# Strassen's seven products also for the last four column blocks of the value matrix, and a ring of output rows one slot shorter

## The chip, the cores and the metric

The kernel runs on one core of a Trainium2 chip. A core has five engines that run their own instruction queues side by side: TensorE (PE; its weight loads are listed as PEld), VectorE (DVE), ScalarE (ACT), GpSimd (POOL) and SyncE (SP, which here issues DMAs). The metric is device time in microseconds (us) of one execution, the median of several runs.

## What is computed

Eight batches, eight heads, 576 positions, head size 64; then a gated layer over 4608 tokens of 512 features, with 1536 hidden features:

```python
scores = q @ k.T / sqrt(64)                  # per batch and head
ret    = scores * Dmat                       # Dmat: gamma_h ** (i - j) for i >= j, else 0
attn   = ret @ v
x      = attn, tokens x 512
gate   = 1 / (1 + exp(-(x @ w_gate)))
val    = x @ w_val
out    = (gate * val) @ w_out
```

The inputs are float32; the kernel multiplies in bfloat16 and adds in float32.

## The kernel before

**The tokens.** The attention is made in steps of 128 tokens. Its output x, transposed, is handled by the gated layer in blocks: 512 tokens at the start, two blocks of 256 (512 and 768 in `BLOCKS`), and seven blocks of 512 from token 1024 on. The change concerns these seven. While the gated layer of one block runs, the attention steps of the next are put between its products.

**The order.** The program is scheduled by hand (`manual_schedule`): each engine takes its instructions in the order in which the program issues them, and an instruction waits by semaphore until its inputs are there and until whatever still reads the place it writes is done.

**Strassen in a 512-token block.** The 1536 hidden features are three units (`u` = 0, 1, 2) of four column blocks of 128 each. For a unit, the product of 512 tokens, 512 features and 512 columns is a 2 x 2 product of quarters. With Strassen's scheme (Winograd's form) it takes seven quarter products instead of eight. A quarter product (`quarter`, `product`, the matmuls on L967) is four matmuls of 128 x 128 by 256 columns. The text names it by kind, unit and number: g16 is gate, unit 1, product 6; w is the value. The two weight-side sums and the difference that a unit needs (`w_sums`) and the token-side sums (`x_sums`) are made ahead.

A unit's products run through three PSUM banks, "a", "g" and "e" (`BANKS`). What happens to them (`quarter`):

- 1 goes into a; ScalarE copies a into g (L994). 2 adds into g, and g leaves as the first quarter of the result.
- 6 adds into a; ScalarE copies a away as u2 (L949). 5 goes into e; ScalarE copies e away as s5 (L949).
- 3 adds into e; VectorE adds e to u2 (L1002). That result leaves as another quarter.
- 7 adds into a; VectorE adds a to s5 (L1005). That result leaves as another quarter.
- 4 adds into a once more, and a leaves as the last quarter.

"Leaves" (L988, L990) is for the gate a sigmoid on ScalarE into the tile `gv`, and for the value a multiplication of `gv` in place: on VectorE where it comes from a bank (products 2 and 4), on GpSimd where it comes from u2 or s5 (products 3 and 7). The leaving of 3 and 7 is put into the list `waiting` and issued only behind the matmuls of the next product, ahead of that product's own work (`settle`).

**Plain products.** Before the change, all three units of the gate and the first two of the value are made like this. The last four column blocks of the value (8 to 11) are made plainly by `value(fc)`: per column block four matmuls of 512 columns (L1016) and one VectorE multiplication (L1019).

**The order of a block** is written out in `ORDER`. Behind a colon stand the sums of finished `gv` quarters (`gsum`) that the output product needs: "0", "1", "2" on VectorE (L909), "t" on GpSimd (L903), and "a", "b" for one half of a unit, four sums each, all on GpSimd. Three quarter products of a block are issued early, in the block before (`EARLY`).

**The output product** (`quarters`, L1074) is again seven products, of 12 matmuls of 256 columns each (1.31 us). The first begins as soon as `ORDER` is through. Behind it comes a group of two attention steps (`slot_of_two`). In it VectorE's two tiny `glance` copies (L698) separate the two halves of the attention values in the same banks: TensorE may begin the second half only behind them. VectorE then masks the next scores (L643).

**Rings.** `ffn_psum` hands out three PSUM banks and `osb` 13 places of 128 x 512 float32, least recently used first; three of the `osb` places are held for weight sums of the value (`value_sums_begin`). Finished output rows wait in `osb`; up to `keeps` = 6 of them stay before the oldest is sent (`stored`, `leave`). `weight_sums` lists the weight-side sums that are issued one by one during the two 256-token blocks, and `PLACES` the in-place differences issued later.

Of the kernel before, what the change touches and what calls it, by code (L numbers as in the profile page):

```python
# [9 lines left out]
FP32 = mybir.dt.float32  # L10
BF16 = mybir.dt.bfloat16
AF = mybir.ActivationFunctionType
ALU = mybir.AluOpType
# [3 lines left out]
def kernel(  # L17
# [19 lines left out]
    nc = tc.nc  # L37
# [4 lines left out]
    P = 128  # L42
    M = H // 2
    NC = (S + P - 1) // P
    NKC = DM // P
    NFC = DFF // P
# [18 lines left out]
    class Ring:  # L65
# [4 lines left out]
            self.held = []  # L70
            self.partly = set()

        def tile(self, shape, dt, tag, name, written=False):
            i = next(x for x in self.order if x not in self.held and not (written and x in self.partly))
            self.partly.discard(i)
            if name.startswith("row"):
                self.partly.add(i)
            self.order.remove(i)
            self.order.append(i)
            self.last = i  # L80
            return self.pool.tile(shape, dt, tag=f"{tag}{i}", name=name)

    ffn_psum = Ring(ffn_banks, 3)
    osb = Ring(osb_pool, 13)

    SUMS = 8
    sum_next = [0]
# [226 lines left out]
    NU = NFC // 4  # L314
    NQ = 2
    wgt_sb = consts.tile([P, 3, NU, 2, 2 * P], BF16)
    wt3_sb = {"g": [wgt_sb[:, i] for i in range(3)]}

    def value_sums_begin():

        wt3_sb["w"] = []
        for i in range(3):
            wt3_sb["w"].append(osb.tile([P, NQ, 2, 2 * P], BF16, tag="osb", name=f"wvt_{i}"))
            osb.held.append(osb.last)

    def w_quarters(kind, u):

# [4 lines left out]
    def w_sums(kind, i, u, eng):  # L332

        a11, a12, a21, a22 = w_quarters(kind, u)
        s1, s2, s4 = (wt3_sb[kind][j][:, u] for j in range(3))
        to, a, b, op = ((s1, a21, a22, ALU.add), (s2, s1, a11, ALU.subtract), (a21, a11, a21, ALU.subtract),
                        (s4, a12, s2, ALU.subtract))[i]
        eng.tensor_tensor(out=to, in0=a, in1=b, op=op)
# [4 lines left out]
    def xT(rows_, cols):  # L343

        t0, n = max(b for b in [(0, 512)] + BLOCKS if b[0] <= cols.start)
        assert cols.stop <= t0 + n
        if t0 not in x_tiles:
            x_tiles[t0] = x_pool.tile([P, M, 512], BF16, tag="x", name=f"xT_{t0}")
        return x_tiles[t0][:, rows_, cols.start - t0:cols.stop - t0]
# [517 lines left out]
                gvs[fc // 4 * 4 + i] = unit[:, i]  # L867
        return gvs[fc]

    keeps = [6]  # L870
    stores = []

    def leave():
# [54 lines left out]
    def quarter_units(gvs, t0):  # L928

        BANKS = {("g", 0): [(tr_psum, "tr"), (pv_psum, "pv"), (qk_psum, "qk")],  # L930
                 ("g", 1): [(qk_psum, "qk"), (ffn_psum, "ffn"), (st_psum, "st")],
                 ("g", 2): [(pv_psum, "pv"), (st_psum, "st"), (tr_psum, "tr")],
                 ("w", 0): [(ffn_psum, "ffn"), (qk_psum, "qk"), (ffn_psum, "ffn")],
                 ("w", 1): [(ffn_psum, "ffn"), (ffn_psum, "ffn"), (ffn_psum, "ffn")]}
        waiting = []

        def settle():
            while waiting:
                waiting.pop(0)()

        def bank(kind, u, i):
            pool, tag = BANKS[kind, u][i]
            more = {"written": True} if pool is ffn_psum and i == 1 else {}
            name = ("gate" if kind == "g" else "w") + "age"[i]
            return pool.tile([P, 2, 256], FP32, tag=tag, name=f"{name}_{t0}_{u}", **more)

        def keep(kind, u, name, ps):
            t = sum_tile([P, 2, 256], FP32, f"{kind}{name}_{t0}_{u}")
            nc.scalar.copy(out=t, in_=ps)  # L949
            return t  # L950

        def right(i):
            x = xT(ALL, slice(t0, t0 + 512))
            t = turned_x[t0] if i > 3 else None
            return {1: lambda: x[:, 0:2, 0:256], 2: lambda: x[:, 2:4, 0:256], 3: lambda: x[:, 2:4, 256:512],
                    4: lambda: t[1][:, 1], 5: lambda: t[0][:, 0], 6: lambda: t[0][:, 1], 7: lambda: t[1][:, 0]}[i]()

        def left(kind, u, i):
            a11, a12, a21, a22 = w_quarters(kind, u)
            t = wt3_sb[kind]  # L960
            return (a11, a12, t[2][:, u], a22, t[0][:, u], t[1][:, u], a21)[i - 1]

        def product(kind, u, i, ps, first):
            w, x = left(kind, u, i), right(i)
            for f in range(2):
                for kc in range(2):
                    nc.tensor.matmul(ps[:, f], lhsT=w[:, kc, f * P:(f + 1) * P], rhs=x[:, kc],  # L967
                                     start=(first and f == 0 and kc == 0), stop=(f == 1 and kc == 1),
                                     skip_group_check=True)

        of = {}

        def quarter(kind, u, i):

            me = of.setdefault((kind, u), {})
            if i == 1:
                gv_tile(gvs, t0, 4 * u)
                me["a"] = bank(kind, u, 0)
            if i == 5:
                me["e"] = bank(kind, u, 2)  # L980
            a, e = me.get("a"), me.get("e")
            product(kind, u, i, {1: a, 6: a, 7: a, 4: a, 5: e, 3: e, 2: me.get("g")}[i], i in (1, 5))
            settle()

            def leaves(r, h, src, eng=nc.vector):
                to = made[t0, u][:, 2 * r:2 * r + 2, h * 256:(h + 1) * 256]
                if kind == "g":
                    nc.scalar.activation(out=to, in_=src, func=AF.Sigmoid)  # L988
                else:
                    eng.tensor_tensor(out=to, in0=to, in1=src, op=ALU.mult)  # L990

            if i == 1:
                me["g"] = bank(kind, u, 1)
                nc.scalar.copy(out=me["g"], in_=a)  # L994
            elif i == 2:
                leaves(0, 0, me["g"])
            elif i == 5:
                me["s5"] = keep(kind, u, "s5", e)
            elif i == 6:
                me["u2"] = keep(kind, u, "u2", a)  # L1000
            elif i == 3:
                nc.vector.tensor_tensor(out=me["u2"], in0=e, in1=me["u2"], op=ALU.add)  # L1002
                waiting.append(lambda: leaves(0, 1, me["u2"], nc.gpsimd))
            elif i == 7:
                nc.vector.tensor_tensor(out=me["s5"], in0=a, in1=me["s5"], op=ALU.add)  # L1005
                waiting.append(lambda: leaves(1, 1, me["s5"], nc.gpsimd))
            else:
                leaves(1, 0, a)
            return 4 * 256

        def value(fc):

            pool, tag = (qk_psum, "qk") if fc < NFC - 2 else (ffn_psum, "ffn")
            ps = pool.tile([P, 512], FP32, tag=tag, name=f"h2_{t0}_{fc}")
            for kc in range(NKC):
                nc.tensor.matmul(ps, lhsT=wv_sb[:, kc, fc * P:(fc + 1) * P], rhs=xT(kc, slice(t0, t0 + 512)),  # L1016
                                 start=(kc == 0), stop=(kc == NKC - 1))
            settle()
            nc.vector.tensor_tensor(out=gvs[fc], in0=gvs[fc], in1=ps, op=ALU.mult)  # L1019
            return 4 * 512  # L1020

        return quarter, value

    EARLY = ((10, "g01"), (13, "g05"), (13, "g02"))
    PLACES = (((1, 1), "g", 0), ((1, 2), "w", 0), ((2, 1), "w", 1), ((2, 2), "g", 1), ((2, 6), "o", 0),
              ((2, 7), "o", 1), ((2, 11), "g", 2), ((2, 45), "o", 2))
    TURN_AT = -1
    CASTS_AT = (5, 32)
    SECOND = 7
    ORDER = ("g06 g11 w05 g03 w01 g15 g16 g12 g07 w06 g13 g21 g17 w03 w11 w07 g04 w02 g14 w04 w16:0t"  # L1030
             " g26:00 w12 w15:01 w17:02 g25 g22 w13 g27 g23 w14:10 v8 v9:1t:2a g24 v10:11 v11:12:2b").split()
    begun = {}

    def gates_early(t0):

        gvs = {}
        begun[t0] = gvs, *quarter_units(gvs, t0)
        for _, x in EARLY:
            yield begun[t0][1](x[0], int(x[1]), int(x[2]))

# [148 lines left out]
    def ffn_units(t0, n, nxt):  # L1189
# [5 lines left out]
        order = steps_of(t0)  # L1195
        if t0 not in begun:
            gvs = {}
            begun[t0] = gvs, *quarter_units(gvs, t0)
        gvs, quarter, value = begun[t0]
        sums = {}  # L1200
        for x in order:
            x, *behind = x.split(":")
            if x[0] == "v":
                cols = value(int(x[1:]))
            else:
                cols = quarter(x[0], int(x[1]), int(x[2]))
            for one in behind:
                u, i = int(one[0]), one[1]
                if u not in sums:
# [238 lines left out]

    weight_sums = [lambda kind=kind, u=u, i=i: w_sums(kind, i, u, nc.vector) for kind, u in (("w", 1), ("g", 2)) for i in (0, 1, 3)]
    weight_sums += [lambda u=u, i=i: wo_sums(i, u, 3) for u in range(3) for i in (0, 1, 3)]  # L1450

    SPARE = {}
    for at, kind, u in PLACES:
# [85 lines left out]
```

## Time and profile before

| what | value |
|---|---|
| three runs | 309.88, 309.88, 310.28 us; median 309.88 |
| span of the profiled execution, first to last instruction | 308.8 us |
| median of the runs less that span | 1.1 us |
| TensorE | busy 299.8 us (97%), 4286 matmuls |
| VectorE | busy 234.6 us (76%), 493 instructions |
| ScalarE | busy 194.0 us (63%), 425 instructions |
| GpSimd | busy 203.0 us (66%), 240 instructions |
| granted TensorE clock | 0.999 on the mean |
| HBM | 37.75 MB read, 9.44 MB written |

The profiled execution's own time is not listed apart from the runs; its span stands beside their median, and the 1.1 us between them are taken as what lies around the span. A row of the table of instruction groups names line, engine, operation and tiles (out<-in), the shape, the count, and behind the bar the busy time and the mean duration of one in ns; then the idle time of that engine just before these instructions, and what ended it. A row of a timeline has the start in us from the span's beginning, the duration, engine, line, operation and tiles, the count (several like instructions are merged into one row) and in brackets the idle time before it. A matmul's duration reaches to the end of its own data, so consecutive matmuls overlap in these rows; the distance of their starts is what one costs. The durations of VectorE and ScalarE overlap with their successors as well, by about 0.1 us.

### The profile page before, as it was taken

To read this page: it belongs to the slowest core of one execution; us is meant where nothing else is said; L and a number is where in the kernel's file an instruction comes from. 1 tells how busy PE (TensorE), PEld (TensorE's weight loads), DVE (VectorE), ACT (ScalarE), POOL (GpSimd) and SP (SyncE) were. 2 spreads that over 40 slices of the span, in tenths; PEclk is the share of its full clock that TensorE was granted. 3 is DMA by queue.
4 is the path that set the end of the run, shared out by engine and by line. 5 is a ranking of instruction groups with operands and counts; after the bars stand their busy time and mean duration, and the time that the engine had idled before them with its cause. 6 is when DMAs were issued, how large, how long until landed. Compare 5 with 4: busy or idle time off the path is not lost. (4 is left out here: it accounts for less than half of the span.)

```text
span 308.8 us, 10424 instructions
## 1 busy us (share of the span) xinstructions
PE 299.8 (97%) x4286; PEld 235.5 (76%) x4286; DVE 234.6 (76%) x493; ACT 194.0 (63%) x425; POOL 203.0 (66%) x240
## 2 busy tenths in 40 slices
PE   7999999999999999999899999999999999999994
PEld 6664456867868778878787788778877887788773
DVE  5956966886898998697769976977699769735943
ACT  6755364446459646964597479746974797459730
POOL 5775654653564899779577977797779707810770
PEclk9999999999999999999999999999999999999999
DMA  7999999997999478993679569948981174003004
GB/s 208 316 370 386 356 302 234 207 194 175 222 210 247 104 180 175 195 310 69 139 163 271 116 138 200 240 110 115 204 211 57 36 230 147 4 24 114 3 1 137
DMA packets 144992, 54.98 MB, mean 178 GB/s; under 512 B 124336, under 2 KB 136880, under 8 KB 144944
## 3 DMA queue, kind: packets, MB, share of 16 engines
q1 hardware_dynamic: 144144, 53.66, 70.6%
q8 instruction: 33, 0.54, 0.7%
q10 hardware_dynamic: 800, 0.66, 0.7%
q14 instruction: 15, 0.12, 0.1%
HBM read 37.75 MB, written 9.44 MB: 153 GB/s over the span
## 5 line engine op out<-in xcount | busy, mean ns | idle before, releaser
L398 POOL TENSOR_TENSOR qk<-k,ktab 128x512 bf16<-128x512 f32 x30 | 32.4, 1080 | 18.4 <-DMA k<-in_k_dram 16.4
L967 PEld LDWEIGHTS <-wg_sb 128*128 128x128 bf16 x336 | 32.9, 98 | 5.5
L1074 PEld LDWEIGHTS <-gsum 128*128 128x128 bf16 x336 | 32.3, 98 | 4.3 <-POOL gsum L909 0.4
L990 POOL TENSOR_TENSOR gv<-gv,wu 128x512 bf16<-128x512 bf16 x14 | 16.3, 1164 | 28.0 <-DVE wu L1002 28.0
L398 POOL TENSOR_TENSOR qk<-q,qtab 128x512 bf16<-128x512 f32 x28 | 30.9, 1102 | 2.8 <-DMA q<-in_q_dram 2.7
L903 POOL TENSOR_TENSOR gsum<-gv 128x512 bf16<-128x512 bf16 (+1 forms) x28 | 27.3, 973 | 5.3 <-DVE gv L990 5.3
L967 PEld LDWEIGHTS <-wgt_sb 128*128 128x128 bf16 x252 | 24.6, 98 | 3.2
L1016 PE MATMUL h<-xT,wv_sb 128*128 128x512 bf16 x112 | 26.5, 379 | 0.0
L1074 PEld LDWEIGHTS <-gv 128*128 128x128 bf16 x240 | 23.0, 98 | 4.3
L967 PE MATMUL gatea<-xsum,wg_sb 128*128 128x256 bf16 x168 | 25.2, 273 | 0.0
L643 DVE TENSOR_TENSOR pt<-row,tri 128x256 bf16<-128x256 f32 x60 | 21.5, 416 | 4.8 <-PE row L636 4.5
L967 PEld LDWEIGHTS <-wv_sb 128*128 128x128 bf16 x224 | 21.9, 98 | 2.5
L712 ACT CAST xT<-val 128x256 bf16<-128x256 f32 x50 | 15.7, 386 | 10.1 <-PE val L670 7.0
L990 POOL TENSOR_TENSOR gv<-gv,ws 128x512 bf16<-128x512 bf16 x14 | 17.1, 1219 | 7.6 <-DVE ws L1005 7.6
L1005 DVE TENSOR_TENSOR gs<-gatea,gs 128x512 f32<-128x512 f32 x21 | 14.4, 688 | 9.7 <-PE gatea L967 8.9
L1002 DVE TENSOR_TENSOR gu<-gatee,gu 128x512 f32<-128x512 f32 x21 | 14.4, 687 | 9.5 <-ACT gateg L994 7.3
L403 POOL CAST v<-v 128x512 bf16<-128x512 f32 x29 | 19.0, 656 | 2.0 <-DMA v<-in_v_dram 2.0
L1019 DVE TENSOR_TENSOR gv<-gv,h 128x512 bf16<-128x512 bf16 x28 | 18.4, 679 | 2.4 <-PE h L1016 2.4
L1016 PEld LDWEIGHTS <-wv_sb 128*128 128x128 bf16 x112 | 10.9, 98 | 10.2
L604 ACT CAST sb<-s 128x256 bf16<-128x256 f32 x46 | 17.5, 421 | 1.3 <-DVE s L765 0.3
L988 ACT ACTIVATE gv<-gs 128x512 bf16<-128x512 f32 x21 | 13.4, 639 | 7.6 <-DVE gs L1005 7.6
L967 PEld LDWEIGHTS <-wvt 128*128 128x128 bf16 x168 | 16.4, 98 | 1.9
(178 smaller groups left out, 828.3 us busy)
## 6 DMA issues: line engine op xcount, KB each, us to landing
k<-in_k_dram SPq DMA_DIRECT2D x26, 256.0 KB, 3.8
q<-in_q_dram SPq DMA_DIRECT2D x26, 256.0 KB, 4.2
v<-in_v_dram SPq DMA_DIRECT2D x26, 256.0 KB, 4.4
out_dram<-ob SPq DMA_DIRECT2D x25, 256.0 KB, 2.6
wg<-in_moe_w_gate_dram SPq DMA_DIRECT2D x12, 256.0 KB, 5.2
wv<-in_moe_w_val_dram SPq DMA_DIRECT2D x12, 256.0 KB, 5.2
wo<-in_moe_w_out_dram SPq DMA_DIRECT2D x12, 256.0 KB, 4.6
v32p<-in_v_dram SPq DMA_DIRECT2D x6, 256.0 KB, 4.5
```

What stands on the lines that cost most here:

```text
L398: eng.tensor_tensor(out=natural_qk[s][:, i].rearrange("p m (y d) -> p y m d", y=2), in0=by_halves(loaded[s][1 - i]), in1=tab, op=ALU.mult)
L403: eng(out=natural["v", s], in_=loaded[s][2])
L604: eng(out=state[key], in_=src)
L643: nc.vector.tensor_tensor(out=probs[s][:, y], in0=row_ps[s][y][:, 0], in1=tri.unsqueeze(1).to_broadcast([P, M, 64]), op=ALU.mult)
L712: nc.scalar.copy(out=x_out(ALL, cols_of(s, i)), in_=x_in(val_ps[s][i], cols_of(s, i)))
L903: nc.gpsimd.tensor_tensor(out=s3, in0=a11, in1=a21, op=ALU.subtract)
L967: nc.tensor.matmul(ps[:, f], lhsT=w[:, kc, f * P:(f + 1) * P], rhs=x[:, kc], start=(first and f == 0 and kc == 0), stop=(f == 1 and kc == ...
L990: eng.tensor_tensor(out=to, in0=to, in1=src, op=ALU.mult)
L1002: nc.vector.tensor_tensor(out=me["u2"], in0=e, in1=me["u2"], op=ALU.add)
L1016: nc.tensor.matmul(ps, lhsT=wv_sb[:, kc, fc * P:(fc + 1) * P], rhs=xT(kc, slice(t0, t0 + 512)), start=(kc == 0), stop=(kc == NKC - 1))
L1019: nc.vector.tensor_tensor(out=gvs[fc], in0=gvs[fc], in1=ps, op=ALU.mult)
L1074: nc.tensor.matmul(ps[:, b], lhsT=left(fp)[:, b * P:(b + 1) * P], rhs=right(fp), start=(first and fp == 0 and b == 0), stop=(fp == NFC // ...
```

## The change

The third unit of the value is also made by seven quarter products (w21 to w27), and `value` is gone. Its banks are two of `qk_psum` for a and e, and for g the `ffn_psum` bank that the second unit's g had. Its three weight sums get a tile of their own (`wvt_last`) and are issued on GpSimd at the end of `weight_sums`; the in-place difference has a place in `PLACES`. `ORDER` is rewritten from w15 on. The sums "a" and "b" of the third unit are replaced by the whole-unit sums 0, 1, 2 on VectorE and t on GpSimd. `osb` has 12 places instead of 13, and `keeps` is 5.

```diff
-        def tile(self, shape, dt, tag, name, written=False):
-            i = next(x for x in self.order if x not in self.held and not (written and x in self.partly))
+        def tile(self, shape, dt, tag, name, written=False, slot=None):
+            i = slot
+            if i is None:
+                i = next(x for x in self.order if x not in self.held and not (written and x in self.partly))
...
-    osb = Ring(osb_pool, 13)
+    osb = Ring(osb_pool, 12)
...
+    wvt_last = consts.tile([P, 3, 2, 2 * P], BF16)
+    wt3_sb["w", NU - 1] = [wvt_last[:, i] for i in range(3)]
...
-    keeps = [6]
+    keeps = [5]
...
-                 ("w", 1): [(ffn_psum, "ffn"), (ffn_psum, "ffn"), (ffn_psum, "ffn")]}
+                 ("w", 1): [(ffn_psum, "ffn"), (ffn_psum, "ffn"), (ffn_psum, "ffn")],
+                 ("w", 2): [(qk_psum, "qk"), (ffn_psum, "ffn"), (qk_psum, "qk")]}
...
+            if (kind, u, i) == ("w", 2, 1):
+                more["slot"] = slot_of["w", 1, 1]
...
-        def value(fc):
-
-            pool, tag = (qk_psum, "qk") if fc < NFC - 2 else (ffn_psum, "ffn")
-            ps = pool.tile([P, 512], FP32, tag=tag, name=f"h2_{t0}_{fc}")
-            for kc in range(NKC):
-                nc.tensor.matmul(ps, lhsT=wv_sb[:, kc, fc * P:(fc + 1) * P], rhs=xT(kc, slice(t0, t0 + 512)),
-                                 start=(kc == 0), stop=(kc == NKC - 1))
-            settle()
-            nc.vector.tensor_tensor(out=gvs[fc], in0=gvs[fc], in1=ps, op=ALU.mult)
-            return 4 * 512
...
-              ((2, 7), "o", 1), ((2, 11), "g", 2), ((2, 45), "o", 2))
+              ((2, 7), "o", 1), ((2, 11), "g", 2), ((2, 14), "w", 2), ((2, 48), "o", 2))
...
     ORDER = ("g06 g11 w05 g03 w01 g15 g16 g12 g07 w06 g13 g21 g17 w03 w11 w07 g04 w02 g14 w04 w16:0t"
-             " g26:00 w12 w15:01 w17:02 g25 g22 w13 g27 g23 w14:10 v8 v9:1t:2a g24 v10:11 v11:12:2b").split()
+             " g26:00 w12 w15:01 w21 g25 w17:02 w26 g22 w13 w22 g27 w25 w14:10 g23 w23:1t g24:11 w27:12 w24:20:21:2t:22").split()
...
+    weight_sums += [lambda i=i: w_sums("w", i, 2, nc.gpsimd) for i in (0, 1, 3)]
```

More of the change, by code (lines that the diff above doesn't have):

```diff
@@ L316 @@
     wgt_sb = consts.tile([P, 3, NU, 2, 2 * P], BF16)
-    wt3_sb = {"g": [wgt_sb[:, i] for i in range(3)]}
+    wt3_sb = {("g", u): [wgt_sb[:, i, u] for i in range(3)] for u in range(NU)}
+    wvt_last = consts.tile([P, 3, 2, 2 * P], BF16)
+    wt3_sb["w", NU - 1] = [wvt_last[:, i] for i in range(3)]
     def value_sums_begin():
-        wt3_sb["w"] = []
         for i in range(3):
-            wt3_sb["w"].append(osb.tile([P, NQ, 2, 2 * P], BF16, tag="osb", name=f"wvt_{i}"))
+            t = osb.tile([P, NQ, 2, 2 * P], BF16, tag="osb", name=f"wvt_{i}")
             osb.held.append(osb.last)
+            for u in range(NQ):
+                wt3_sb.setdefault(("w", u), []).append(t[:, u])
     def w_quarters(kind, u):
@@ L334, in w_sums @@
         a11, a12, a21, a22 = w_quarters(kind, u)
-        s1, s2, s4 = (wt3_sb[kind][j][:, u] for j in range(3))
+        s1, s2, s4 = wt3_sb[kind, u]
         to, a, b, op = ((s1, a21, a22, ALU.add), (s2, s1, a11, ALU.subtract), (a21, a11, a21, ALU.subtract),
@@ L933, in quarter_units @@
                  ("w", 0): [(ffn_psum, "ffn"), (qk_psum, "qk"), (ffn_psum, "ffn")],
-                 ("w", 1): [(ffn_psum, "ffn"), (ffn_psum, "ffn"), (ffn_psum, "ffn")]}
+                 ("w", 1): [(ffn_psum, "ffn"), (ffn_psum, "ffn"), (ffn_psum, "ffn")],
+                 ("w", 2): [(qk_psum, "qk"), (ffn_psum, "ffn"), (qk_psum, "qk")]}
         waiting = []
+        slot_of = {}
         def settle():
@@ L943, in bank @@
             more = {"written": True} if pool is ffn_psum and i == 1 else {}
+            if (kind, u, i) == ("w", 2, 1):
+                more["slot"] = slot_of["w", 1, 1]
             name = ("gate" if kind == "g" else "w") + "age"[i]
-            return pool.tile([P, 2, 256], FP32, tag=tag, name=f"{name}_{t0}_{u}", **more)
+            t = pool.tile([P, 2, 256], FP32, tag=tag, name=f"{name}_{t0}_{u}", **more)
+            if pool is ffn_psum:
+                slot_of[kind, u, i] = pool.last
+            return t
         def keep(kind, u, name, ps):
@@ L959, in left @@
             a11, a12, a21, a22 = w_quarters(kind, u)
-            t = wt3_sb[kind]
-            return (a11, a12, t[2][:, u], a22, t[0][:, u], t[1][:, u], a21)[i - 1]
+            s1, s2, s4 = wt3_sb[kind, u]
+            return (a11, a12, s4, a22, s1, s2, a21)[i - 1]
         def product(kind, u, i, ps, first):
@@ L1009, in quarter @@
             return 4 * 256
-        def value(fc):
-            pool, tag = (qk_psum, "qk") if fc < NFC - 2 else (ffn_psum, "ffn")
-            ps = pool.tile([P, 512], FP32, tag=tag, name=f"h2_{t0}_{fc}")
-            for kc in range(NKC):
-                nc.tensor.matmul(ps, lhsT=wv_sb[:, kc, fc * P:(fc + 1) * P], rhs=xT(kc, slice(t0, t0 + 512)),
-                                 start=(kc == 0), stop=(kc == NKC - 1))
-            settle()
-            nc.vector.tensor_tensor(out=gvs[fc], in0=gvs[fc], in1=ps, op=ALU.mult)
-            return 4 * 512
-        return quarter, value
+        return quarter
     EARLY = ((10, "g01"), (13, "g05"), (13, "g02"))
     PLACES = (((1, 1), "g", 0), ((1, 2), "w", 0), ((2, 1), "w", 1), ((2, 2), "g", 1), ((2, 6), "o", 0),
-              ((2, 7), "o", 1), ((2, 11), "g", 2), ((2, 45), "o", 2))
+              ((2, 7), "o", 1), ((2, 11), "g", 2), ((2, 14), "w", 2), ((2, 48), "o", 2))
     TURN_AT = -1
@@ L1036, in gates_early @@
         gvs = {}
-        begun[t0] = gvs, *quarter_units(gvs, t0)
+        begun[t0] = gvs, quarter_units(gvs, t0)
         for _, x in EARLY:
@@ L1197, in ffn_units @@
             gvs = {}
-            begun[t0] = gvs, *quarter_units(gvs, t0)
-        gvs, quarter, value = begun[t0]
+            begun[t0] = gvs, quarter_units(gvs, t0)
+        gvs, quarter = begun[t0]
         sums = {}
@@ L1202, in ffn_units @@
             x, *behind = x.split(":")
[L1203 to L1206, printed above, removed]
+            cols = quarter(x[0], int(x[1]), int(x[2]))
             for one in behind:
```

## The prediction

> **What bounds the kernel now.** I read the page first, then the chain of waits, then the timeline of each engine in one 512-token block (185 to 207 us; the other blocks repeat it every 31 us).
>
> ```profile
> PE 299.8 (97%) x4286; PEld 235.5 (76%) x4286; DVE 234.6 (76%) x493; ACT 194.0 (63%) x425; POOL 203.0 (66%) x240
> ...
> PEclk9999999999999999999999999999999999999999
> ...
> L1016 PE MATMUL h<-xT,wv_sb 128*128 128x512 bf16 x112 | 26.5, 379 | 0.0
> ...
> L1019 DVE TENSOR_TENSOR gv<-gv,h 128x512 bf16<-128x512 bf16 x28 | 18.4, 679 | 2.4 <-PE h L1016 2.4
> ```
>
> TensorE has work 97% of the span, at full clock, and the rows that the change touches never wait. The chain that ended last is TensorE nearly throughout, and prices both forms of the product:
>
> ```profile
> 291.00 0.44 PE wa L967 x4
> 291.44 1.73 PE h L1016 x8
> ```
>
> A quarter product (4 matmuls of 256 columns) takes 0.44 us, more exactly 0.4375 (ten quarters from 279.16 to 283.58, less a 0.05 wait). Eight plain matmuls of 512 columns take 1.73, so the 16 of a block take 3.46.
>
> Every TensorE instruction saved is therefore worth its time, if no new wait appears. So I looked at how close the block comes to waiting. ("Quarter w27" below is the value, unit 2, product 7.)
>
> ```profile
> 189.24 0.60 PE L967 MATMUL wa<-xsum,wvt 128*128 128x256 bf16 x4
> 189.73 0.60 PE L967 MATMUL gatee<-xT,wgt_sb 128*128 128x256 bf16 x4
> ```
>
> The first is w06, the second g13, which adds into a bank whose product 5 ScalarE must first have copied out:
>
> ```profile
> 189.10 0.58 ACT L949 COPY gs<-gatee 128x512 f32<-128x512 f32 x1
> ```
>
> The copy ends at 189.68 and g13 starts at 189.73, 0.05 late. So product 3 does wait for the copy of product 5, and likewise product 4 must wait for VectorE's addition that reads the bank after product 7. In the old order three or more products always lie between 7 and 4 of a unit. This, and the length of VectorE's queue, is what the new order must be measured against:
>
> ```profile
> 192.78 0.60 PE L967 MATMUL wg<-xT,wv_sb 128*128 128x256 bf16 x4
> ```
> ```profile
> 193.42 0.69 DVE L990 TENSOR_TENSOR gv<-gv,wg 128x512 bf16<-128x512 bf16 x1 [0.18 <-PE wg L967]
> ...
> 198.40 0.68 DVE L1005 TENSOR_TENSOR gs<-gatea,gs 128x512 f32<-128x512 f32 x1
> 198.99 0.68 DVE L1002 TENSOR_TENSOR gu<-gatee,gu 128x512 f32<-128x512 f32 x1
> 199.59 0.68 DVE L990 TENSOR_TENSOR gv<-gv,wa 128x512 bf16<-128x512 bf16 x1
> 200.19 0.42 DVE L909 TENSOR_TENSOR gsum<-gv 128x512 bf16<-128x512 bf16 x1
> ...
> 202.80 0.83 DVE L909 TENSOR_TENSOR gsum<-gsum,gv 128x512 bf16<-128x512 bf16 x1
> ...
> 204.16 0.92 DVE L909 TENSOR_TENSOR gsum<-gv,gsum 128x512 bf16<-128x512 bf16 x1
> 204.99 0.21 DVE L698 COPY glance<-val 128x1 f32<-128x1 f32 x2
> ```
>
> What the reader is to take: a quarter that starts at t can be read from t + 0.64 (192.78 to 193.42). A VectorE operation on a bank takes 0.69 until its result is there, and the next may start 0.61 after it; a sum takes 0.42 (next after about 0.40). From 196 on VectorE hardly pauses.
>
> **Removed and added on TensorE.** 16 matmuls at 216 ns (3.46) become 28 at 109 ns (7 x 0.4375 = 3.06): 0.40 per block, 2.8 us over seven blocks. That is the whole gain.
>
> **Work on the other engines, per block.** ScalarE: three more copies of 0.59, 1.8, in a stretch of 19.2 us where it is busy for 14.6 (windows view); no cost by their number. GpSimd: eight half sums of 0.68 to 0.76 (5.7) and nothing else go; two multiplications of 1.16 to 1.22 and one whole third sum of 1.20 come: 2.2 less, no cost. VectorE: four multiplications (2.7) go; two additions, two multiplications (2.7) and three sums (1.8) come: 1.8 more, at the end of the stage, where it is already full. Once only: three GpSimd sums of about 1.2 during the second 256-token block, where GpSimd waits 1.1 to 1.9 us for each key load (16.4 us in all), and one VectorE sum of 0.42 at the start of the first big block. I put these at nothing; uncovered, they cost 4 us at most. The shorter ring: a block takes four rows, and the store of a reused slot is still issued a block (about 30 us) before the reuse; 2.6 us to landing. Nothing.
>
> **The walk through the new order.** Until w15 (starts 195.40) both orders are alike. Then, at 0.4375 each, on the block's own clock: w21 195.84, g25 196.28, w17 196.71, w26 197.15, g22 197.59, w13 198.03, w22 198.46, g27 198.90, w25 199.34, w14 199.77, g23 200.21, w23 200.65.
>
> VectorE's queue: addition of w13 at 198.03 + 0.64 = 198.67; multiplication of w22 at 199.28; addition of g27 at 199.89, there at 200.58; multiplication of w14 at 200.50, sum 10 at 201.11, addition of g23 at 201.51. No gap.
>
> First new wait: the sigmoid of g27's addition stands ahead of the copy of w25 on ScalarE. Sigmoid at 200.61, copy 0.50 later at 201.11, there at 201.70. w23 adds into the bank being copied: 201.74 instead of 200.65, a wait of 1.09. Behind it TensorE has only w23, g24, w27, w24, in order.
>
> Second new wait: w27 then starts at 202.62 and w24 follows directly, on the same bank. The addition of w27 is ready at 203.26, behind w23's addition (202.38) and sum 11 (202.99 to 203.39): it runs from 203.39 to 204.08, and w24 starts at 204.12 instead of 203.05. A wait of 1.07, of which 0.64 + 0.69 + 0.04 - 0.44 = 0.93 is there even with an empty VectorE queue.
>
> w24 ends at 204.55; before, the stage ended at 202.79. So 2.16 - 0.40 = +1.76 per block, +12.3 over seven. Bounds of the two waits: 1.9 (0.93 and a little less queue) to 2.56 (sum 11 stretched as the 0.83 row).
>
> The Trainium skill's "Perfetto Trace Analysis" (Matmuls) asks that independent groups rotate through PSUM banks, so that emptying one overlaps the next group. Read for this change, that page says that w27 and w24 cannot overlap; it has no price, and none is used.
>
> **After the stage.** VectorE still owes w24's multiplication (204.76 to 205.45) and sums 20, 21, 22, ahead of the two glance copies that hold back the second half of the attention values on TensorE. Before, TensorE was ready for them 2.33 us after the stage's end and waited about 0.1. Now it is ready at 204.55 + 2.33 = 206.88. Sum 20 needs GpSimd's last multiplication: GpSimd takes w23's from 203.13 to 204.35 and w27's to about 205.55. Then 20 at 205.6, 21 at 206.0, 22 at 206.4, glances at 206.75, TensorE at 207.0: no loss, the lower end. But the two long sums above (0.83, 0.92) were issued beside a running GpSimd sum:
>
> ```profile
> 202.69 0.67 POOL L909 TENSOR_TENSOR gsum<-gsum,gv 128x256 bf16<-128x256 bf16 x1
> ...
> 204.12 0.67 POOL L909 TENSOR_TENSOR gsum<-gv,gsum 128x256 bf16<-128x256 bf16 x1
> ```
>
> GpSimd's ended at 203.36 and 204.79, VectorE's 0.27 and 0.29 later; it seems to stand until the other is through. Third sum 2t (1.20, from about 205.9) would hold 21 to 207.3, and 22 and the glances to 207.9: about 1.0 lost. Another 0.3 of GpSimd delay makes 1.3, the upper end. I take 0.8, near the case with 2t first, since both rows speak for it. Six blocks have attention steps behind them: +4.8.
>
> The Trainium skill's "SBUF — State Buffer" (Who interferes with whom) calls this an exclusive lock: whichever of the two starts first holds the ports for its whole instruction. The rows above agree; by that rule alone the sum would have 1.0 in place of 0.8, 328 us in all.
>
> **Sum.** 12.3 + 4.8 = 17.1. The profiled span is 308.8; the three runs' median is 309.88, so 1.1 lie around the span and stay. 309.9 + 17.1 = 327.0.
>
> **Rivals.**
> - All cover holds: only the 0.40 per block counts, 309.9 - 2.8 = 307.1. For it: TensorE waits nowhere over 0.06 us in these stages now, and the other engines have idle time on the page. Against: w24 needs the bank that VectorE reads 0.64 after w27's start. It decides at one point: whether w24's first matmul may start before that addition ends. The g13 row says no. 0.06.
> - The waits eat just the gain, within 0.6 us of now: needs 0.40 of waits per block, under half of the 0.93. 0.02.
> - Only w24's wait binds: VectorE is not late, so ScalarE's copy of w25 is in time. 7 x (0.93 - 0.40) = +3.7, 313.6. Against: from 198.67 the queue is gapless on rows of the same kind. 0.09.
> - The clock falls in these pauses. If half clock held from w23 to the end of the first output product (4 x 0.44 + 1.31 = 3.1 us), each block would lose 3.1 more, 21 in all: 348. Against: TensorE stood for 0.9 us at 148, and the windows view shows clock 1.00 there and behind it. 0.03. The Trainium skill's "TensorE: Matmul & The Clock Gate" (Part 1) has the clock fall after an idle window of about 3.4 us, longer than either pause; no run here shows it.
>
> **How the numbers follow.** The forecast has 0.80. Its range: 7 x (1.9 - 0.40) + 0 = 10.5, so 320.4; 7 x (2.56 - 0.40) + 6 x 1.3 = 22.9, so 332.8, both ends improbable together at the top: 320.4 to 332. About 0.2% (0.6 us) is what a measurement of this kernel can tell from no change. Faster 0.06, same 0.02, slower 0.92.
>
> **What would show it.** Right: in each 512-token block a pause of about 1.1 us ahead of product 3 of w2, released by ScalarE's copy, and one of about 1.1 ahead of its product 4, released by VectorE's addition; glance waits of 0 to 1.3 in six blocks; no plain value matmuls left in these blocks. Wrong: product 4 following product 7 at 0.44, or pauses under 0.5; a TensorE clock under 1; waits at w21 or w26, which I have just in time; GpSimd casts or stores that hold TensorE up.

## The result and the profile after

The changed kernel takes 336.87 us against 309.88: a ratio of 1.088 (95% interval 1.084 to 1.092), 27.0 us slower, where 17.1 slower was forecast (range 320.4 to 332). The profiled execution took 337.4 us with a span of 335.7, 26.9 more than before.

From the page of the changed kernel, the engines, the clock and one group:

```profile
PE 301.5 (90%) x4361; PEld 245.1 (73%) x4370; DVE 251.4 (75%) x515; ACT 204.5 (61%) x446; POOL 198.2 (59%) x208
...
PEclk9999999999999979999999999999999999999999
...
L979 PE MATMUL wa<-xsum,wv_sb 128*128 128x256 bf16 x168 | 25.2, 272 | 8.0 <-DVE ws L1017 8.0
```

The same group and TensorE's wait for the glances in the kernel before:

```profile
L967 PE MATMUL wa<-xsum,wv_sb 128*128 128x256 bf16 x112 | 16.8, 273 | 0.0
```
```profile
PE val L670 <- DVE glance L698: 0.3, 1, 0.3
```

TensorE now has work for 90% of the span instead of 97%, its clock fell once, and a matmul group that never waited has 8.0 us of waiting in front of it. Lines have moved: the quarter products are L979 (were L967), the output products L1075, ScalarE's copies L961, VectorE's additions L1014 and L1017, its sums L914. Who TensorE waited for (us in total, times, longest):

```profile
PE val L675 <- DVE glance L703: 10.3, 7, 1.8
PE wa L979 <- DVE ws L1017: 8.0, 7, 2.5
PE we L979 <- ACT ws L961: 6.5, 7, 0.9
PE wa L979 <- ACT wg L1006: 1.4, 1, 1.4
```

The second and third rows are the two pauses of the walk, once per block. One of the seven glance waits, 0.5 by starts, stands in the kernel before too. The view counts a matmul's modelled end as work; measured by the distance of starts, each is a little longer. TensorE's timeline at the end of one block:

```profile
215.17 0.60 PE L979 MATMUL gatee<-xT,wgt_sb 128*128 128x256 bf16 x4
216.69 0.60 PE L979 MATMUL we<-xT,wvt_last 128*128 128x256 bf16 x4 [0.93 <-ACT ws L961]
217.13 0.60 PE L979 MATMUL gatea<-xsum,wg_sb 128*128 128x256 bf16 x4
217.56 0.60 PE L979 MATMUL wa<-xsum,wv_sb 128*128 128x256 bf16 x4
219.08 0.60 PE L979 MATMUL wa<-xsum,wv_sb 128*128 128x256 bf16 x4 [0.91 <-DVE ws L1017]
219.51 1.47 PE L1075 MATMUL qa<-wo_sb,gv 128*128 128x256 bf16 x12
```

g23 starts at 215.17 and w23 1.52 later instead of 0.44: a pause of 1.08 (1.09 in the exact stamps). w27 starts at 217.56 and w24 1.52 later: 1.08 (1.07). And behind the stage, VectorE's and GpSimd's timelines of the same block:

```profile
219.78 0.69 DVE L1002 TENSOR_TENSOR gv<-gv,wa 128x512 bf16<-128x512 bf16 x1
220.78 0.43 DVE L914 TENSOR_TENSOR gsum<-gv 128x512 bf16<-128x512 bf16 x1 [0.31 <-POOL gv L1002]
221.24 1.26 DVE L914 TENSOR_TENSOR gsum<-gsum,gv 128x512 bf16<-128x512 bf16 x1
222.53 1.15 DVE L914 TENSOR_TENSOR gsum<-gv,gsum 128x512 bf16<-128x512 bf16 x1
223.60 0.21 DVE L703 COPY glance<-val 128x1 f32<-128x1 f32 x2
```
```profile
220.82 1.39 POOL L908 TENSOR_TENSOR gsum<-gv 128x512 bf16<-128x512 bf16 x1
222.18 1.22 POOL L403 TENSOR_TENSOR qk<-k,ktab 128x512 bf16<-128x512 f32 x1
```

Sum 20 takes 0.43. Sum 21 takes 1.26 and ends at 222.50, 0.29 behind the end of GpSimd's third sum (222.21). Sum 22 takes 1.15 and ends at 223.68, 0.28 behind the end of the key cast (223.40). The glances come at 223.60, and TensorE, ready at 221.9, goes on at 223.86.

The last of the six blocks with such a wait is a check on this, for there GpSimd has no cast left behind its third sum. VectorE's sums 21 and 22 in it, and GpSimd's third sum:

```profile
290.12 1.26 DVE L914 TENSOR_TENSOR gsum<-gsum,gv 128x512 bf16<-128x512 bf16 x1
291.41 0.43 DVE L914 TENSOR_TENSOR gsum<-gv,gsum 128x512 bf16<-128x512 bf16 x1
```
```profile
289.70 1.39 POOL L908 TENSOR_TENSOR gsum<-gv 128x512 bf16<-128x512 bf16 x1
```

Sum 21 is held up as before, sum 22 is not, and TensorE waits 1.39 in place of 1.92.

Where the 26.9 us are (pauses from distances of starts, less what the same place cost before):

| place | us |
|---|---|
| two pauses of 1.09 and 1.07 in seven blocks, less 0.40 of matmul time each | 12.3 |
| glance waits: 1.93, 1.92, 1.92, 2.02, 1.92, 1.39, less 0.45 before | 10.7 |
| first of the seven blocks alone: 1.5 ahead of w06, 1.6 more than the others ahead of w24 | 3.1 |
| 3.4 us at half clock (119.7 to 123.1) | 1.7 |
| up to the last output product before that block (86.80 to 87.49) | 0.7 |
| a pause of 1.05 at 148 in the old trace that the new one has not | -1.05 |
| sum | 27.4 |

### The profile page after: what moved, and what is told of

Its sections match the earlier page's. It is cut to its first block, busy times and chain, and to the rows that moved or that the text cites. A ratio compares the mean times of both kernels' runs of the same rounds, so it can differ in the third digit from the quotient of the medians.

```text
span 335.7 us, 10614 instructions
## 1 busy us (share of the span) xinstructions
PE 301.5 (90%) x4361; PEld 245.1 (73%) x4370; DVE 251.4 (75%) x515; ACT 204.5 (61%) x446; POOL 198.2 (59%) x208
## 5 line engine op out<-in xcount | busy, mean ns | idle before, releaser
L403 POOL TENSOR_TENSOR qk<-k,ktab 128x512 bf16<-128x512 f32 x30 | 33.3, 1109 | 17.9 <-DMA k<-in_k_dram 13.8
L1002 POOL TENSOR_TENSOR gv<-gv,wu 128x512 bf16<-128x512 bf16 x21 | 24.8, 1179 | 31.6 <-DVE wu L1014 31.1
L979 PEld LDWEIGHTS <-wv_sb 128*128 128x128 bf16 x336 | 32.8, 98 | 12.9 <-issue 9.2
L1075 PEld LDWEIGHTS <-gsum 128*128 128x128 bf16 x336 | 33.0, 100 | 4.5
L979 PEld LDWEIGHTS <-wg_sb 128*128 128x128 bf16 x336 | 32.9, 98 | 4.0
L1002 POOL TENSOR_TENSOR gv<-gv,ws 128x512 bf16<-128x512 bf16 x21 | 26.5, 1261 | 12.2 <-DVE ws L1017 12.2
L403 POOL TENSOR_TENSOR qk<-q,qtab 128x512 bf16<-128x512 f32 x28 | 31.7, 1132 | 2.4 <-DMA q<-in_q_dram 2.4
L979 PE MATMUL wa<-xsum,wv_sb 128*128 128x256 bf16 x168 | 25.2, 272 | 8.0 <-DVE ws L1017 8.0
L908 POOL TENSOR_TENSOR gsum<-gv 128x512 bf16<-128x512 bf16 x21 | 27.0, 1286 | 6.7 <-DVE gv L1002 6.0
L931 POOL TENSOR_TENSOR xsum<-xT 128x512 bf16<-128x512 bf16 x6 | 6.9, 1158 | 38.1 <-ACT xT L717 32.4
L979 PEld LDWEIGHTS <-wgt_sb 128*128 128x128 bf16 x252 | 24.6, 98 | 3.3
L1075 PEld LDWEIGHTS <-gv 128*128 128x128 bf16 x240 | 23.1, 99 | 3.2
L979 PE MATMUL gatea<-xsum,wg_sb 128*128 128x256 bf16 x168 | 25.2, 273 | 0.0
L1017 DVE TENSOR_TENSOR gs<-gatea,gs 128x512 f32<-128x512 f32 x21 | 14.4, 688 | 9.2 <-PE gatea L979 8.5
L1014 DVE TENSOR_TENSOR gu<-gatee,gu 128x512 f32<-128x512 f32 x21 | 14.4, 688 | 9.0 <-ACT gateg L1006 7.2
L979 PEld LDWEIGHTS <-wvt 128*128 128x128 bf16 x168 | 16.4, 98 | 3.4 <-issue 1.5
L1000 ACT ACTIVATE gv<-gu 128x512 bf16<-128x512 f32 x21 | 13.4, 639 | 8.7 <-DVE gu L1014 8.7
L1017 DVE TENSOR_TENSOR ws<-wa,ws 128x512 f32<-128x512 f32 x21 | 14.5, 688 | 5.0 <-PE wa L979 4.9
```

The costliest lines, as they stand in the source:

```text
L403: eng.tensor_tensor(out=natural_qk[s][:, i].rearrange("p m (y d) -> p y m d", y=2), in0=by_halves(loaded[s][1 - i]), in1=tab, op=ALU.mult)
L908: nc.gpsimd.tensor_tensor(out=s3, in0=a11, in1=a21, op=ALU.subtract)
L931: eng.tensor_tensor(out=to, in0=a, in1=b, op=ALU.subtract)
L1075: nc.tensor.matmul(ps[:, b], lhsT=left(fp)[:, b * P:(b + 1) * P], rhs=right(fp), start=(first and fp == 0 and b == 0), stop=(fp == NFC // ...
```

## The experiments

The revised theory has three parts. Inside the stage, VectorE's queue sets both pauses, and the banks only pass it on. Behind the stage, VectorE's sums stand still while GpSimd runs, whatever it runs. The first block has a cause of its own. The rivals are in the expectations. The ratios are to the kernel before, run again beside each experiment.

**e1: take away the first pause alone.**

```diff
-w21 g25 w17:02 w26 g22 w13 w22 g27 w25 w14:10 ...
+w21 w25 g25 w17:02 w26 g22 w13 w22 g27 w14:10 ...
```

> w25 moved from behind g27 to directly behind w21, all else as in the changed kernel, so that ScalarE copies its bank long before w23. Theory (one shared VectorE queue sets both pauses): the pause of 1.09 us ahead of w23 goes, but the VectorE queue was never idle because of it, so it comes back in the pause ahead of w24, which grows from 1.07 to 2.2 or 2.3 us. Per block 0 to 0.15 us more, total 336 to 338.5. Rival (each pause costs by itself and is worth its length when taken away): 7 x 1.09 = 7.6 us less, 329.

Measured 339.03 us (ratio to before 1.093, 1.089 to 1.097). Waits of TensorE:

```profile
PE wa L979 <- DVE ws L1017: 16.0, 7, 4.1
PE val L675 <- DVE glance L703: 9.1, 7, 1.9
```

The waits for ScalarE's copy (6.5 us) are gone, and those for VectorE doubled from 8.0 to 16.0: ahead of w24 2.15 us in each of the last five blocks. Taking away a pause of 1.09 gave nothing: the two were 2.16 together, and the one left is 2.15. It is VectorE's queue that shows, at whichever of the two places comes first. The queue was not wholly gapless, though. In the changed kernel VectorE stands idle for 0.36 behind the first pause; in e1 it does not, but moving w25 ahead also puts the products behind it, and with them VectorE's work, 0.44 later, which takes up that gain. The half us over the expected band fits the clock, which fell three times in the profiled execution (13.7 us at half speed, against 3.4 in the changed kernel).

**e2: take away the second pause alone.**

```diff
-... w25 w14:10 g23 w23:1t g24:11 w27:12 w24:20:21:2t:22
+... w25 w14:10 w27 g23 w23:1t g24:11 w24:12:20:21:2t:22
```

> w27 moved from between g24 and w24 to ahead of g23, so that three products lie between w27 and w24 on the same bank; sum 12 goes behind w24. Theory (VectorE's queue at the end of the stage is the limit, the bank only shows it): the pause ahead of w24 goes and the one ahead of w23 falls to 0.6 us, but the first output product then waits about 0.8 us for w24's multiplication and the glance wait grows from 1.9 to about 3.5 us. Per block about 0.6 us more, total about 340 (337 to 342). Rival (product 4 right behind product 7 is the cause): the pause of 1.07 goes and nothing takes its place, 7 x 1.07 = 7.5 us less, 329.

Measured 353.76 us (1.141, 1.137 to 1.145). The pauses were as expected: none ahead of w24 but in the first block, 0.66 ahead of w23, 0.80 in the first output product, 3.1 at the glance (about 3.5 expected). The time was missed by 12 us, and the windows view says why (us, busy time of PE, PEld, DVE, ACT, POOL, then the clock):

```profile
191.80:195.20 3.40, 1.54 (x114) 1.25 (x115) 2.27 (x5) 0.57 (x1) 3.32 (x4) 1.00 0.02 5
195.20:198.60 3.40, 2.26 (x26) 1.64 (x26) 3.33 (x10) 0.65 (x2) 2.41 (x3) 0.50 0.12 27
198.60:202.10 3.50, 3.50 (x18) 2.52 (x17) 0.67 (x2) 2.47 (x9) 0.00 (x0) 0.51 0.89 143
202.10:205.50 3.40, 3.40 (x141) 2.95 (x140) 1.43 (x6) 1.78 (x5) 0.00 (x0) 1.00 0.63 144
```

From within the glance wait on the clock is halved for 6.8 us, in five blocks, and for 3.4 in the sixth. What runs there takes twice as long.

**e3: the sums 20, 21, 22 on GpSimd.**

```diff
-gv_sum(made[t0, u], sums[u], slice(0, 2), int(i), nc.vector)
+gv_sum(made[t0, u], sums[u], slice(0, 2), int(i), nc.gpsimd if u == 2 else nc.vector)
```

> The three sums 20, 21, 22 of the third unit on GpSimd instead of VectorE; order and everything else as in the changed kernel. Theory (the glance copies stand behind sums that GpSimd's third sum and the next cast hold up): the glance waits fall from 1.9 us to 0.3 or less in the six blocks that have them, about 10 us less, 326.5; the two pauses of 1.1 us ahead of w23 and w24 stay. Rival (the glance is late because w24 itself is late, whatever the sums do): no change over 2 us, 335 to 337. Second rival (the output products then wait for the slower GpSimd sums instead): 2 to 6 us less only, with waits of TensorE at L1075 on GpSimd.

Measured 328.02 us (1.059, 1.053 to 1.065), 8.9 less than the changed kernel:

```profile
PE wa L979 <- DVE ws L1017: 8.0, 7, 2.5
PE we L979 <- ACT ws L961: 6.5, 7, 0.9
PE wa L979 <- ACT wg L1006: 1.4, 1, 1.4
...
PE val L675 <- DVE glance L703: 0.7, 2, 0.4
```

The glance waits fall from 10.3 to 0.7 and all others stay. Both rivals fall. One of the six blocks has an output wait of 0.68 with no releaser that the trace names.

**e9: only the third sum 2t moved, to VectorE.** It asks what on GpSimd holds the sums up.

```diff
-    def third_sum(unit, t, pairs):
+    def third_sum(unit, t, pairs, eng=nc.gpsimd):
...
-        nc.gpsimd.tensor_tensor(out=s3, in0=a11, in1=a21, op=ALU.subtract)
+        eng.tensor_tensor(out=s3, in0=a11, in1=a21, op=ALU.subtract)
...
-                    third_sum(made[t0, u], sums[u], slice(0, 2))
+                    third_sum(made[t0, u], sums[u], slice(0, 2), nc.vector if u == 2 else nc.gpsimd)
```

> Against the changed kernel: only the third unit's third sum (2t) on VectorE, in its place between 21 and 22, instead of GpSimd. Theory (VectorE's sums stand still while any GpSimd instruction that reads its operands is running, a cast as well as a sum; casts simply follow on GpSimd earlier): the sums 20 to 22 again end about 0.28 us behind the end of a GpSimd instruction, and the glance wait stays at 1.7 to 2.8 us: 336 to 341. Rival (2t is what holds them up, or the number of sums on VectorE does not matter): the glance wait falls under 0.6, 8 us less, 329.

Measured 345.01 us (1.107, 1.101 to 1.113), 4 over the band; the clock fell three times here too. VectorE's and GpSimd's timelines behind a stage:

```profile
223.67 1.25 DVE L914 TENSOR_TENSOR gsum<-gv 128x512 bf16<-128x512 bf16 x1 [0.31 <-POOL gv L1002]
224.94 1.15 DVE L914 TENSOR_TENSOR gsum<-gsum,gv 128x512 bf16<-128x512 bf16 x1
226.02 0.82 DVE L908 TENSOR_TENSOR gsum<-gv 128x512 bf16<-128x512 bf16 x1
226.76 0.41 DVE L914 TENSOR_TENSOR gsum<-gv,gsum 128x512 bf16<-128x512 bf16 x1
```
```profile
223.59 1.04 POOL L403 TENSOR_TENSOR qk<-k,ktab 128x512 bf16<-128x512 f32 x1
224.59 1.22 POOL L403 TENSOR_TENSOR qk<-q,qtab 128x512 bf16<-128x512 f32 x1
225.76 0.80 POOL L408 CAST v<-v 128x512 bf16<-128x512 f32 x1
```

With 2t out of the way the casts come at once, and each holds up one sum: the first three end at 224.92, 226.09 and 226.84, which is 0.29, 0.28 and 0.28 behind the ends of the casts. The fourth, with GpSimd idle, takes 0.41. In four of the six blocks the glance wait grew to 2.5 or 2.6 us; it is 1.30 in the first. In the last, where no cast follows, nothing holds the four sums up, and the wait falls to 0.76:

```profile
295.44 0.42 DVE L914 TENSOR_TENSOR gsum<-gv 128x512 bf16<-128x512 bf16 x1 [0.30 <-POOL gv L1002]
295.89 0.42 DVE L914 TENSOR_TENSOR gsum<-gsum,gv 128x512 bf16<-128x512 bf16 x1
296.24 0.42 DVE L908 TENSOR_TENSOR gsum<-gv 128x512 bf16<-128x512 bf16 x1
296.57 0.42 DVE L914 TENSOR_TENSOR gsum<-gv,gsum 128x512 bf16<-128x512 bf16 x1
```

So casts hold the sums up as the third sum did; it need not be the third sum.

**e4 and e7: the first block.** e4 makes the three new weight sums on VectorE; e7 changes `CASTS_AT = (5, 32)` to `(5, 33)`.

> The three weight sums of the value's third unit on VectorE (as all other weight sums) instead of GpSimd; all else as in the changed kernel. Theory (on GpSimd they stand behind casts that wait for loads, run only when the first 512-token block has begun, and slow VectorE's sums and the casts there): the waits that only this block has (1.5 us ahead of w06, 1.6 us more than the others ahead of w24) go, 2 to 3.5 us less, 333.5 to 335. Rival (they are hidden, and that block is late for another reason): within 1 us of the changed kernel's 336.9.

> One number against the changed kernel: the second of the two extra casts of the first 512-token block is issued one product later (33 instead of 32), which puts it behind w13's multiplication on GpSimd instead of ahead of it. Theory (the three casts, 2.6 us, stand ahead of that multiplication there, sum 10 waits for it, and with it VectorE's queue and w24): the pause ahead of w24 in the first block falls from 2.7 to the 1.07 of the others, 1.6 us less; with it the fall of the clock behind it may go, another 1.6 us less: 333.5 to 335.5. Rival (that block is late for its weight sums and extra differences): no change.

e4: 337.11 us (1.086, 1.083 to 1.089), no change. The pause ahead of w06 fell only from 1.5 to 1.1, the one ahead of w24 stayed at 2.67. The theory of the weight sums falls but for the 0.4 ahead of w06. e7: 337.33 us (1.087, 1.083 to 1.090), no change either, but its reason holds as far as it goes. GpSimd's timeline of the changed kernel in that block:

```profile
107.71 1.04 POOL L403 TENSOR_TENSOR qk<-k,ktab 128x512 bf16<-128x512 f32 x1
108.71 1.04 POOL L403 TENSOR_TENSOR qk<-q,qtab 128x512 bf16<-128x512 f32 x1
109.70 0.61 POOL L408 CAST v<-v 128x512 bf16<-128x512 f32 x1
110.27 1.16 POOL L1002 TENSOR_TENSOR gv<-gv,wu 128x512 bf16<-128x512 bf16 x1
```

The three casts stand ahead of w13's multiplication, and VectorE's sum 10 waits 1.97 for that. One product later they stand behind it, and the pause ahead of w24 falls from 2.68 to 1.22 (1.07 expected). But now the later multiplications are behind the casts, and the glance wait of that block grows from 1.93 to 3.03. The clock still fell once, in another block.

**e5: the shorter ring alone, in the kernel before** (12 places, `keeps` 5).

> The kernel before with only the ring changed: 12 output rows instead of 13, five stay instead of six. Theory (rows are sent a whole block before their place is used again): within 0.6 us of before. Rival (the shorter ring is what delays the first blocks, by 0.7 us before the first Strassen block and 1.1 to 1.5 us ahead of w06 in it): 1 to 2.5 us slower than before.

309.88 us, ratio 0.999 (0.996 to 1.002): nothing, as predicted.

**e8: e2's move on top of e3.**

> The kernel e3 (sums 20, 21, 22 on GpSimd) with w27 moved ahead of g23, as in e2. Theory (moving w27 was bad in e2 only because VectorE's queue then ran into the first output product and the glance, and the clock fell behind that; without the three sums little of that is left): pause ahead of w24 gone, 0.66 us ahead of w23, 0.8 us in the first output product, glance under 0.4: about 0.6 us per block less than e3, 323 to 325. Rival (the order of e2 is bad by itself): slower than e3's 328.

322.98 us (1.041, 1.036 to 1.047), 5 less than e3. The same move that cost 17 us in e2 now gains: the glance waits are gone (0.3 in all), and in the profiled execution the clock did not fall. Per block 2.16 of pauses became 0.66 + 0.80. So 0.70 of them went with the order, in which w24 stands right behind w27, and 1.46 stayed.

**e6 and e10: can the smaller matmuls be had without the pauses?** e6 has e3's edit, e4's edit and this order; e10 puts sum 11 behind w24.

```diff
-... w04 w16:0t g26:00 w12 w15:01 w21 g25 w17:02 w26 g22 w13 w22 g27 w25 w14:10 g23 w23:1t g24:11 w27:12 w24:20:21:2t:22
+... w04:00 w16 g26 w12 w15:0t:01 w17 w21:02 g25 w13 w26 g27 w14:10:1t w25 g23 w27 g22 w23 w22:11 g24 w24:12:20:21:2t:22
```

> A version meant to keep the 28 smaller matmuls without the pauses: sums 20, 21, 22 on GpSimd; the order from w04 on rearranged so that in unit 2 of the value five products lie between products 5 and 3 ... counted as w25 g23 w27 g22 w23, two between 5 and 3 with ScalarE's queue short there, and four between 7 and 4; sums moved with them; the weight sums on VectorE. Theory (the pauses are VectorE's and ScalarE's queues, so an order that feeds them evenly has none): pauses ahead of w23 and w24 under 0.1 us, up to 0.2 us of wait in the first output product, no glance wait over 0.3, no fall of the clock; 309 to 313. Rival (the third unit's work cannot be hidden in any order, VectorE being full at the end of the stage): 318 or more.

> Against the combined version e6: sum 11 behind w24 instead of w22, so that w24's multiplication on VectorE no longer stands behind it. Theory: the wait of 0.33 us in the first output product goes in the seven blocks, but sums 11 and 12 then meet GpSimd's multiplications and hold the glance copies up by 0.1 to 0.4 in six: 310.5 to 313. If VectorE's sums are not held up: 0.33 x 7 = 2.3 us less than 312.85, 310.5, the same as before.

e6: 312.85 us (1.007, 1.004 to 1.011). The time is in the expected band, and the rival falls. The pauses of the stage are gone outside the first block, and the first output product waits 0.33 for w24's multiplication (0.2 expected). From one block's first output product to the next it needs 30.64 us where before needed 30.86 (264.78 - 234.14 and 264.52 - 233.66): 0.22 of the 0.40 arrive. The rest of the kernel loses that again: the first block, two pauses of 0.32 and 1.03 whose releaser the trace does not name, and the tail behind the last block's first output product (14.96 against 13.63), where one wait of 0.53 is for a sum that GpSimd now makes. e10: 316.43 us (1.016, 1.012 to 1.021), over its band: the 0.33 is gone, but sums 11 and 12 meet GpSimd and the glance waits become 0.8 to 1.0 in six blocks. No version run here beats the kernel before.

## Why the prediction was right or wrong

- **The gain:** right in size. Without its pauses a block takes 30.4 us (34.43 from 253.96 to 288.39, less 1.92, 1.09 and 1.07) where it took 30.9.
- **The walk through the order:** right to 0.01 us. Pauses of 1.09 and 1.07, released by ScalarE's copy of w25 and VectorE's addition of w27; +12.3 in all. e1 adds what the walk implied: VectorE's nearly gapless queue is behind both pauses, and taking one away alone is worth nothing. e8 adds that 0.70 of the 2.16 was the order's.
- **After the stage:** the term that was mis-sized. It was put at 0.8 per block, 4.8 in all; it measured 10.7, with 1.92 in a typical block, above its upper end of 1.3. Sum 21 was held by 2t as described. Two steps failed. First, what follows 2t on GpSimd was put at nothing, though the third sum frees GpSimd 2.7 us behind the stage (before, the half sums kept it until 4.8 behind it) and the key cast follows without a pause. Sum 22 took 1.15 for it; in the last block, without the cast, it took 0.43. That is 0.53 of wait (1.92 less 1.39) in five blocks, 2.7 us. GpSimd casts that hold TensorE up stood in the list of what would show the prediction wrong, without a price. Second, the case with 2t alone was put too low: 0.8, where the last block shows 1.39, over the upper end by itself. Of these 0.59, 0.2 is the choice of 0.8 below the case's own 1.0. Most of the rest is on GpSimd: w27's multiplication and 2t, put at 1.20 each, took 1.33 and 1.39, each beside a sum on VectorE. e9 shows that the casts alone hold the sums up, e3 that the term goes when the sums leave VectorE. The Trainium skill's "SBUF — State Buffer" (Who interferes with whom) says that a VectorE instruction with two SBUF inputs contends with a GpSimd instruction that reads SBUF. The casts of e9 agree (0.28 to 0.29 behind each end).
- **"Once only, at nothing":** wrong by 3.1 in the first block and 0.7 ahead of it. Of the 3.1, the 1.6 ahead of w24 come from the casts that `CASTS_AT` issues by their place in an order that had become longer (e7), a moved step that the prediction did not look at. Two of the three weight sums ran inside that block (at 92.79 and 94.20), not ahead of it as was put, but they are not the cause of most of it (e4). What makes w06 late by 1.1 to 1.5, and what the 0.7 is, was not settled: VectorE's in-place differences there take up to 1.37 beside GpSimd's work.
- **The rivals:** full cover, the break-even and "only w24's wait" all fell. The falling clock, given 0.03 as a cause of its own, came on top: once in the profiled execution (1.7 us). The reason given against it, that 0.9 us at 148 left the clock at 1.00, says nothing of longer pauses. The idle window of about 3.4 us of the Trainium skill's "TensorE: Matmul & The Clock Gate" (Part 1) differs from these runs, and the runs decide: here windows with 1.9 to 2.1 us of pauses were followed by falls, though not all of them, as the last section shows.
- **The shorter ring:** right, nothing (e5). ScalarE's heavier load: nothing by its amount either; of the waits that every block has, only the copy of w25 is ScalarE's, as walked. GpSimd's lighter load cost nothing by its amount, but what it let come earlier did: the key cast above.

## What to carry to other kernels

When the bound engine runs without a pause, walk every queue that feeds it through the new order instruction by instruction: shares of busy time said that there was room, and the queue said that there was none. Removing one wait of a full queue moved the wait (e1, e2, e7, e10). Taking three sums off that queue removed the wait behind the stage (e3), and with it a better order gained too (e8, e6). When an engine is relieved, look at what it does next and with whom that collides: here GpSimd's third sum held up one sum of VectorE, and the cast that came early behind it held up the next.

## What the runs showed of the hardware

- **The clock falls for pauses well under 3.4 us.** Falls last 3413 ns or a multiple of it and begin on a grid of that period. They were set beside the pauses of TensorE (gaps of over 0.15 us by distances of starts) in the changed kernel and all ten experiments. Windows of that grid at full clock with 2.15 us or more of pauses in them were followed by half clock in 7 of 7 cases, those with 1.9 to 2.1 in about a third, and those with less in none. The edges move by 0.1 to 0.2 us with how short a gap is counted. Where a pause lies matters, since one that is split over two windows counts in each for its part alone. That does not settle all of it: two glance waits of the changed kernel lay whole inside a window, one in its first block, which was followed by a fall, and one of 1.92 at 256.4, which was not, with TensorE busy for nearly the same time:

```profile
116.30:119.70 3.40, 1.65 (x102) 1.47 (x87) 3.37 (x7) 0.82 (x3) 3.40 (x4) 1.00 0.81 184
119.70:123.10 3.40, 3.40 (x19) 2.44 (x17) 2.36 (x7) 1.83 (x8) 0.43 (x1) 0.50 0.52 119
```
```profile
256.25:259.65 3.40, 1.66 (x60) 1.44 (x50) 3.36 (x9) 0.65 (x2) 3.34 (x4) 1.00 0.02 5
259.65:263.05 3.40, 3.40 (x82) 2.91 (x82) 1.45 (x4) 2.91 (x9) 0.00 (x0) 1.00 0.37 84
```

- **A sum held up by GpSimd ends 0.28 to 0.29 us behind it**, whatever its own start. That holds for all 181 sums of `gv` quarters on VectorE that took over 0.5 us in the twelve traces (277 to 286 ns behind the end of a GpSimd instruction). That instruction may be a sum, a multiplication, a multiplication by a table or a plain cast.
